# A recurrent attention and a full attention on one core: new order of the segments, paired projection tails, a rebuilt prologue

## The chip, the core and the metric

The kernel runs on one core of one Trainium2 chip. The metric is the time of one execution on the device in microseconds (us). The kernel before takes 1615.6 us (median of 4 runs, 1615.0 to 1619.6).

## The reference, cut to what matters

```python
# A: 64 segments of 32 tokens, one after the other; 8 memory tokens go from each to the next
for s in range(n_seg):
    h = concat([mem, x[s*32:(s+1)*32]])              # 40 tokens x 576
    q, k, v = h @ Wq, h @ Wk, h @ Wv                 # 32 heads of 128
    p = softmax(where(mask, q @ k.T * scale, -1e9))
    o = (p @ v) @ Wo
    mem = o[:8]; outs.append(o[8:])
# B: full attention over all 2048 tokens, 32 heads of 18
b = softmax(q @ k.T * scale) @ v @ wo
# gate
return g * a + (1 - g) * b,  g = sigmoid((x * gate_w).sum(-1))
```

A is a chain: a segment's memory tokens are known only when the segment before is done. B is a heap of independent work: 512 *steps*, each of 4 concurrent score matmuls, an exponential over 128 x 2048 elements and 4 concurrent value matmuls. The kernel weaves B's steps into A's segments, so that the engines have something to do while A's chain waits.

The last 8 tokens of a segment depend on no memory, so their queries, keys and values can be made early. These *last tokens* are done for 16 segments at a time, in 24 units, two of which (2.2 us) go into a segment; four times (for segments 0, 16, 32 and 48), so that none is left to do in the last 16 segments. Every fourth segment has *group work* in those places instead, the output rows of four segments.

## The kernel before

Each segment is a list of names, which are the matmul groups, copies and activations in the order of issue. `B` issues a step's scores and the values of the step before, `E` the exponential; `Q0` to `V1` are the six projections, `t` transposes, `S` scores of A, `x n p l r m` the parts of its softmax, `w` the weighing, `a` the output projection, `f` and `ht` the fold into the memory, `F0` to `F2` the places for last tokens or group work, `c...` and `o...` copies out of PSUM, `v0 v1` the stores of the values. `/` and `:` are places where B's divisions go.

```python
ORDERS = {
    7: """
    Q0 cQ0 K0 B E : cK0 / K1 tq0 tk0 pq0 V0 cK1 B E : pk0 Q1 S0 cV0 v0 cQ1 x0 tk1 n0 B E : tq1 pk1
    V1 pq1 p0 cV1 v1 l0 r0 / S1 m0 B F1 w00 x1 n1 o00 F2 cF1 p1 w01 E : B l1 cF2 o01 r1 m1 E : F0
    a00 w10 cF0 w11 B E : o10 o11 ol a01 a10 a11 B / E : h0 g0 h1 g1 f0 ht0 f1 ht1 og oh
    """.split(),
    8: """
    Q0 B E : V0 cQ0 K0 cV0 v0 B / cK0 E : tq0 pq0 Q1 tk0 pk0 cQ1 B / E : S0 K1 tq1 x0 cK1 B n0 tk1 E
    : V1 pk1 pq1 p0 cV1 v1 S1 l0 r0 x1 / B E : F0 m0 n1 w00 o00 F1 cF0 p1 w01 o01 cF1 l1 r1 m1 B F2
    a00 cF2 w10 o10 w11 E : B E : o11 ol a01 a10 h0 a11 g0 B h1 g1 f0 E : f1 ht0 ht1 oh og
    """.split(),
}
...
LOAD_LAST = "r1"       # in the last segment the loads of the last phase are issued behind this name
...
width = 8 if s >= n_seg - eights else 7      # 28 segments of seven steps, then 36 of eight
```

A projection is five rows of four concurrent matmuls. The fifth row has only 64 of 128 input rows filled, the rest is zero:

```python
def project(x, w, b, k):
    pv = bank(k, [P, 512], FP32, "pvv")
    for c in range(NF + 1):                   # 4 full chunks of 128 and the tail
        for j in range(4):
            rw, cc = w_slice(w, c, (2 * (j // 2) + b) * 1024 + (j % 2) * 512, 512)
            nc.tensor.matmul(pv[32 * j:32 * j + 32, :], lhsT=ht[:, cc, :], rhs=rw,
                             start=(c == 0), stop=(c == NF), tile_position=(0, 32 * j))
```

PSUM is tight: B's scores have four of the eight banks in one buffer, its sums one, and all of A's groups share three, by a table (`BANKS`) that goes with each order. A step's scores therefore can't start before the exponential of the step before has read the buffer.

The softmax here doesn't subtract the row's maximum and nothing guards it: scores larger than these inputs give would overflow.

## Time and profile before

The profiled execution spans 1613.9 us. Its stages, with the lines of the profile, stand in the prediction.

### The profile page before, as it was taken

The numbers are of one execution on the slowest core, as the hardware profiler recorded it, in microseconds if no ns is written. First come the engines' busy times: TensorE is split into PE (matmuls) and PEld (weight loads), VectorE is DVE, ScalarE is ACT, GpSimd is POOL, SyncE is SP. The second block draws the span as 40 slices with busy tenths as digits, with TensorE's granted clock in tenths as the row PEclk, the third lists the DMA queues.
The fourth block names the chain that finished last, engine by engine and source line by source line (L and its number), as shares of the span: only waits on it lengthen the run. The fifth ranks groups of instructions, "written<-read, shape, count | busy, mean of one in ns | idle before, by whom it ended". The sixth has DMA issues, their size and how long they took to land.

```text
span 1613.9 us, 57766 instructions
## 1 busy us (share of the span) xinstructions
PE 1476.7 (91%) x25082; PEld 782.0 (48%) x25082; DVE 960.0 (59%) x2355; ACT 1139.8 (71%) x981; POOL 338.4 (21%) x731
## 2 busy tenths in 40 slices
PE   6598899999999999999999999999999989998997
PEld 3434444555454444555454445555554444444445
DVE  2233666666566666666566666666666656565656
ACT  2165577777677767777677777777777777788774
POOL 6311211213131031302121211212121212120131
PEclk9899999999999999999999999999999999999999
DMA  7788322212122121212122121212221121211125
GB/s 200 235 291 290 100 65 64 49 42 52 45 50 53 32 53 38 61 36 49 43 43 60 38 50 40 57 39 45 51 53 35 30 48 34 45 34 35 29 59 162
DMA packets 209865, 114.39 MB, mean 71 GB/s; under 512 B 159491, under 2 KB 197251, under 8 KB 208019
## 3 DMA queue, kind: packets, MB, share of 16 engines
q1 hardware_dynamic: 188971, 58.40, 16.1%
q0 software_dynamic: 19696, 50.02, 9.9%
q8 instruction: 196, 3.21, 0.9%
q10 hardware_dynamic: 944, 2.29, 0.4%
q14 instruction: 58, 0.48, 0.1%
HBM read 60.94 MB, written 36.10 MB: 60 GB/s over the span
## 4 chain that ended last, share of the span: by engine, by line
PE 69%; ACT 11%; DVE 11%; DMA 4%; issue 2%; SPq 1%; POOL 1%; DVEq 0%; ACTq 0%; POOLq 0%
PE pvv L755 27%; ACT etb L257 9%; PE sb L238 8%; PE ob L222 7%; PE pt L782 5%; PE pv L326 4%; PE psh L800 3%; PE acc L643 3%; PE pso L838 3%; PE pv L313 2%; DVE hl L657 2%; PE pq L420 2%; DVE hl L654 2%; DVE ot L850 2%; ACT rq L830 2%
## 5 line engine op out<-in xcount | busy, mean ns | idle before, releaser
L257 ACT ACTIVATE etb<-sb 128x2048 bf16<-128x2048 f32 x512 | 959.6, 1874 | 341.9 <-PE sb L238 341.1
L767 DVE CAST tm<-pvv 128x512 bf16<-128x512 f32 x384 | 264.4, 689 | 175.1 <-PE pvv L755 174.2
L755 PEld LDWEIGHTS <-ht 128*32 128x32 bf16 x7680 | 185.8, 97 | 183.7 <-DVE ht L891 14.1
L238 PE MATMUL sb<-qch,kch 32*128 32x512 bf16 x2048 | 203.2, 386 | 38.5 <-ACT etb L257 36.7
L222 PE MATMUL ob<-etb,vch 128*32 128x512 bf16 x2048 | 205.9, 392 | 3.9 <-DVE tq L159 3.9
L850 DVE CAST ot<-pso 128x320 bf16<-128x320 f32 x256 | 120.7, 488 | 104.2 <-PE pso L838 99.9
L643 PE MATMUL acc<-wo,ot 128*32 128x384 bf16 (+1 forms) x4096 | 159.7, 291 | 5.4 <-DVE ot L850 3.3
L755 PE MATMUL pvv<-wq_m,ht 128*32 128x512 bf16 x2048 | 134.2, 382 | 13.0 <-DVE ht L891 8.3
L755 PE MATMUL pvv<-wk_m,ht 128*32 128x512 bf16 x2048 | 134.9, 384 | 0.0
L755 PE MATMUL pvv<-wv_m,ht 128*32 128x512 bf16 x2048 | 134.3, 382 | 0.0
L643 PEld LDWEIGHTS <-ot 128*32 128x32 bf16 x4096 | 105.2, 98 | 46.5 <-DVE ot L850 12.8
L700 POOL DMA_DIRECT2D a_dram<-rl x186 | 92.6, 506 | 162.4 <-DVE rl L695 143.3
L238 PEld LDWEIGHTS <-kch 32*128 32x128 bf16 x2048 | 61.2, 91 | 128.5 <-issue 107.9
L857 POOL COPY otl<-ot 128x256 bf16<-128x256 bf16 x64 | 25.9, 405 | 445.6 <-DVE ot L850 445.6
L222 PEld LDWEIGHTS <-vch 128*32 128x32 bf16 x2048 | 52.9, 93 | 120.6 <-issue 116.0
L782 PE MATMUL pt<-ident,tm 128*128 128x128 bf16 x1024 | 96.8, 221 | 0.8 <-DVE tm L767 0.8
L790 DVE COPY kt<-pt 128x512 bf16<-128x512 bf16 x128 | 54.0, 422 | 69.4 <-PE pt L782 69.0
L838 PE MATMUL pso<-et,v_sb 64*128 64x40 bf16 x2048 | 81.4, 178 | 14.9 <-DVE hll L657 4.7
L838 PEld LDWEIGHTS <-v_sb 64*128 64x128 bf16 x2048 | 62.8, 93 | 62.4 <-issue 49.5
L654 DVE CAST hl<-acc 128x384 bf16<-128x384 f32 (+1 forms) x128 | 57.9, 452 | 58.1 <-PE acc L643 57.8
L782 PEld LDWEIGHTS <-tm 128*128 128x128 bf16 x1024 | 57.8, 98 | 67.0 <-issue 49.4
L826 ACT ACTIVATE lt<-pss 128x320 f32<-128x320 f32 x128 | 56.0, 438 | 43.2 <-PE pss L822 32.8
(141 smaller groups left out, 1847.4 us busy)
## 6 DMA issues: line engine op xcount, KB each, us to landing
v_sb<-tm SPq DMA_DIRECT2D x512, 32.0 KB
wo<-in_A_Wo_dram POOLq DMA_DIRECT2D x4, 1152.0 KB, 9.7
wv_m<-in_A_Wv_dram POOLq DMA_DIRECT2D x4, 1024.0 KB, 8.0
wq_m<-in_A_Wq_dram POOLq DMA_DIRECT2D x4, 1024.0 KB, 9.1
wk_m<-in_A_Wk_dram POOLq DMA_DIRECT2D x4, 1024.0 KB, 8.0
xl<-qld SPq DMA_DIRECT2D x64, 64.0 KB
xl<-kld SPq DMA_DIRECT2D x64, 64.0 KB
v_sb<-vld SPq DMA_DIRECT2D x128, 32.0 KB
```

What stands on the lines that cost most here:

```text
L222: nc.tensor.matmul(ob[32 * j:32 * j + 32, :], lhsT=vc[:, o + 32 * j:o + 32 * j + 32], rhs=et4[:, j, :], start=(kb == 0), stop=(kb == NKB - 1),
L238: nc.tensor.matmul(sb[:, j, :], lhsT=kc[32 * j:32 * j + 32, o:o + P], rhs=qch[gq][32 * j:32 * j + 32, :], start=True, stop=True, tile_posi ...
L257: nc.scalar.activation(out=before[:, :, :], in_=sb[:, :, :], func=ACT.Exp, scale=scale_b)
L326: nc.tensor.matmul(pv[:, o:o + P], lhsT=lw, rhs=xlb[:, cc, :], start=(c == 0), stop=(c == NF))
L643: nc.tensor.matmul(acc[32 * j:32 * j + 32, 0:d1 - d0], lhsT=o[:, h, 0:CT], rhs=wo[:, h, d0:d1], start=(b == 0 and i == 0), stop=(b == 1 an ...
L654: nc.vector.tensor_copy(out=hl[:, 0, d0:d1], in_=acc[:, 0:d1 - d0])
L700: eng.dma_start(out=rows4[m, seg - LO:seg, i * n:(i + 1) * n], in_=rl[32 * i + m * LO:32 * i + (m + 1) * LO, :],)
L755: nc.tensor.matmul(pv[32 * j:32 * j + 32, :], lhsT=ht[:, cc, :], rhs=rw, start=(c == 0), stop=(c == NF), tile_position=(0, 32 * j),)
L767: nc.vector.tensor_copy(out=sbt[x][:, :], in_=ps[x][:, :])
L782: nc.tensor.transpose(out=pt[:, which, :, :, :].rearrange("p j (u i) t -> p j u i t", i=4)[:, :, :, i, :], in_=sbt[x][:, i * Dh:(i + 1) * Dh],
L838: nc.tensor.matmul(pso[:, i * L:(i + 1) * L], lhsT=v_sb[64 * jj:64 * jj + 64, b * 1024 + i * Dh:b * 1024 + (i + 1) * Dh], rhs=et[64 * jj:6 ...
L850: nc.vector.tensor_copy(out=ot[:, j * HG:(j + 1) * HG, :].rearrange("p h t -> p (h t)"), in_=ps["o", b, jj][:, 0:W8],)
```

## The change

Its intent: let PE do less (three tails in place of six), fill the prologue, put eight-step segments where there are last tokens, and give the last 16 segments, which have none, an order of their own. The diff, cut to its core (not shown: key and query storage by block, hence plain loads of 18 rows a head; the same value matmuls in four column tiles; the new bank tables; setup moved earlier):

```diff
+        def project_tails(two):
+            two = [(x, w, b, begin(x)) for x, w, b in two]
+            for j in range(4):
+                for x, w, b, first in two:
+                    t, r = w_tail(w, columns(b, j), 512)
+                    nc.tensor.matmul(
+                        ps[x][32 * j:32 * j + 32, :],
+                        lhsT=ht[TL * r:TL * r + TL, NF + r, :],
+                        rhs=t[TL * r:TL * r + TL, :],
+                        start=first, stop=(not first),
+                        tile_position=(TL * r, 32 * j), ...
+                    )
...
-        if spare[0] >= 1.8:
-            spare[0] -= 1.8
+        if spare[0] >= 2.15:
+            spare[0] -= 2.2
...
-    for kb in range(NKB):
+    for kb in range(NKB // 2):
         project_vb(1, kb, 3)
-    for blk in (1, 6, 2, 7, 3, 8):
+    for i, blk in enumerate((1, 6, 2, 7, 3, 8)):
         for t in range(NQC):
             project_qk(blk, t, 0)
             between(1.1)
-        store_qk(blk, range(GB))
+            if i > 0:
+                some_tokens()
+            else:
+                for kb in range(NKB // 2 + 2 * t, NKB // 2 + 2 * t + 2):
+                    project_vb(1, kb, 3)
+        store_qk(blk)
...
+        8: """
+        Q0 B T0 K1 E : / cQ0 T1 cK1 B Q1 E : K0 B V0 cQ1 cK0 T2 tk0 E : tq0 B V1 / cV0 v0 pk0 E : pq0
+        tk1 tq1 cV1 v1 pq1 S0 pk1 B x0 / F1 E : n0 S1 p0 x1 cF1 n1 l0 F2 p1 r0 m0 w00 B cF2 l1 o00 r1 F0
+        m1 w01 w11 cF0 o01 E : w10 o11 o10 ol a00 B a01 E : a10 h0 a11 B g0 h1 f0 g1 ht0 f1 ht1 E : og
+        oh
+        0: """
+        / Q0 T0 B K0 cQ0 Q1 E : T1 cK0 B cQ1 E : K1 V0 cK1 B T2 E : V1 tk0 / / cV0 v0 B E : cV1 v1 tq0
+        pk0 tk1 pq0 tq1 S0 pk1 x0 pq1 S1 n0 F1 p0 x1 l0 cF1 F2 n1 p1 B r0 m0 cF2 l1 F0 cF0 r1 m1 w00 w01
+        E : w10 o00 o01 w11 o10 a00 o11 ol B a01 h0 E : g0 a10 a11 h1 g1 B f0 ht0 E : f1 ht1 og oh
...
-    LOAD_LAST = "r1"
+    LOAD_LAST = [n for n in ORDERS[0] if n[0] in "QKVT"][-1]      # V1
...
-        width = 8 if s >= n_seg - eights else 7
+        width = 8 if s < wides else 7 if s < n_seg - SG else 0     # 41 of eight, 7 of seven, 16 of the third
```

`T0`, `T1`, `T2` are the paired tails. The new seven-step order is left out here.

## The prediction

> **What bounds the kernel now.** I read the page first (engine shares, the chain that ended last), then the busy time by stage, then the PE's own timeline in one segment and in the prologue. The page says that the matmul engine is the bound, with short hand-overs to ScalarE and VectorE:
>
> ```profile
> PE 1476.7 (91%) x25082; PEld 782.0 (48%) x25082; DVE 960.0 (59%) x2355; ACT 1139.8 (71%) x981; POOL 338.4 (21%) x731
> ...
> PE 69%; ACT 11%; DVE 11%; DMA 4%; issue 2%; SPq 1%; POOL 1%; DVEq 0%; ACTq 0%; POOLq 0%
> ```
>
> By stage (first number the stretch, then the busy time of each engine, granted clock, share of the DMA engines, GB/s):
>
> ```profile
> 53.30:85.70 32.40, 16.44 (x176) 11.68 (x174) 5.53 (x14) 2.59 (x7) 5.44 (x15) 0.74 0.85 277
> 85.70:174.60 88.90, 74.99 (x709) 38.57 (x712) 39.45 (x71) 54.44 (x29) 15.14 (x27) 0.98 0.78 260
> 174.60:789.10 614.50, 577.59 (x10386) 307.41 (x10386) 388.77 (x962) 433.70 (x364) 130.21 (x284) 0.99 0.22 52
> 789.10:1213.00 423.90, 409.66 (x7279) 213.82 (x7283) 265.53 (x663) 327.13 (x266) 87.23 (x190) 1.00 0.21 47
> 1213.00:1558.30 345.30, 314.99 (x5746) 160.32 (x5747) 210.20 (x537) 274.45 (x225) 55.47 (x130) 1.00 0.17 35
> ```
>
> The prologue ends at 174.6, when the first projection of segment 0 starts; 29 of the 512 big exponentials lie before it. Then come 28 segments of seven steps (rows 174.6 to 789.1), and 36 of eight. The median seven-step segment takes 21.35 us, an eight-step one that also computes last tokens (up to 1213) 22.43, one without them 21.47; segments 0 to 62 take 1383.7 together, and segment 63 with the ending 55.6. So a segment with one step fewer is hardly shorter, and one without last tokens (2.2 us of matmuls less) gains only 1 us: the work is badly spread, heavy segments fill PE, light ones wait.
>
> The PE timeline of segment 36 gives the prices (start, duration, line, tile, instructions):
>
> ```profile
> 969.32 0.39 PE L755 MATMUL pvv<-wq_t,ht 128*32 128x512 bf16 x4
> 969.64 0.40 PE L238 MATMUL sb<-qch,kch 32*128 32x512 bf16 x4
> 969.97 0.40 PE L222 MATMUL ob<-etb,vch 128*32 128x512 bf16 x4
> 970.19 1.04 PE L755 MATMUL pvv<-wv_m,ht 128*32 128x512 bf16 x16
> 971.05 0.39 PE L755 MATMUL pvv<-wv_t,ht 128*32 128x512 bf16 x4
> 971.27 1.04 PE L755 MATMUL pvv<-wk_m,ht 128*32 128x512 bf16 x16
> ```
>
> Start to start, four concurrent 512-wide matmuls take 0.22 us where the next has the same array shape (971.05 to 971.27), and 0.32 where it has another (969.32 to 969.64). A change of shape costs some 0.105 us. Four rows of a projection take 0.86.
>
> In the prologue PE stands still before it starts the second half of B's values, because the staging buffers' stores stand behind weight loads and per-head stores:
>
> ```profile
> 55.37 7.51 PE L447 MATMUL pvb<-wb,xT 128*128 128x288 bf16 x60
> 78.84 4.73 PE L447 MATMUL pvb<-wb,xT 128*128 128x288 bf16 x20 [15.96 <-DVE xn L291]
> ```
>
> **What the Trainium skill says.** "TensorEngine Tiling (Array Packing)", Tiling Modes, Key Properties: changing the tiling mode, not just the tile, drains TensorE. This trace agrees: 0.105 us a change, as above. The same page, Available Configurations, lists eight independent tiles of 64x32; the paired tails need exactly that, and nothing in this trace uses it. The same page, Gotcha 1, asks that different row tiles write different banks; in all three new bank tables the two projections of a pair do. "ScalarE: Activation LUTs", What ACT_TABLE_LOAD costs, gives 186 ns + 0.833 ns an element, 1892 ns for 2048; the trace has a mean of 1874.
>
> **The change part by part.**
>
> *Paired tails.* A projection's last 64 rows were padded to 128, so six tails of a segment cost six rows of 0.212. Now two projections share the array, upper and lower 64 rows: three rows. That saves 3 x 0.212 = 0.64 us a segment on PE. Each pair adds a shape change or so, up to 3 x 0.105; the sums in four column tiles ([...]in the shape of their neighbours) and the new orders take back more than that.
>
> *Count of PE work.* I listed the groups of each order, priced each by start-to-start distances of the trace (row 0.212; step two rows; four transposes 0.22; scores 0.43 per half; weighing 0.2 per group; output projection 0.65 and 0.33; fold 0.45; last-token unit 1.1) and counted shape changes. Before: seven steps with last tokens 16.8 + 29 x 0.105 = 19.85; eight with them 17.2 + 34 x 0.105 = 20.8; eight without 15.0 + 32 x 0.105 = 18.35. Measured were 21.35, 22.43 and 21.47: 1.5, 1.6 and 3.1 more, waits for DVE and ACT and what the prices miss. After: eight with last tokens 16.55 + about 31 x 0.105 = 19.9; seven with them 16.1 + 28 x 0.105 = 19.05; seven without 13.93 + 26 x 0.105 = 16.7.
>
> *Which segments.* Steps between projections come now each 2.2 units of cost (48 x 1.1 / 2.2 = 24), not 1.8 (29). So 65 - 24 = 41 segments have eight steps, and they come first; 7 have seven; the last 16 use the third order, seven steps without last tokens. Five more eight-step segments is what the shorter prologue costs. The light work now goes where PE has less to do.
>
> *Segment times.* Eight steps: 19.9 plus 1.2 (1.6 before; the order was tuned anew) = 21.1. Seven: 20.4. Last 16: PE needs only 16.7, but a step cannot follow the one before faster than 2.43 us (the pace in the prologue with one projection in between: 88.90 to 91.27 and the like: scores 0.45, exponential 1.87, hand-over), since the scores have one buffer. Seven of those are 17.0; with 1.5 for ACT's six small operations (2.7 us a segment, partly in the gaps) and the chain through the memory I take 18.5, and 20.4 for the every fourth segment that projects the last tokens of four. Segments 0 to 62: 41 x 21.1 + 7 x 20.4 + 4 x 20.4 + 11 x 18.5 = 865 + 143 + 82 + 203 = 1293; 10 us for half-clock stretches and hiccups (the trace has five stretches of 3.4 us at half clock within segments, which cost half of it, some 8 us) make 1303, against 1383.7.
>
> *Prologue.* Up to 53 it stays, minus the pads (a 4 us wait in the chain at 19.5), plus four early weight pieces. Per-head stores become one store a block; the loads become four of 18 rows. Only eight of B's second value blocks come before the first step, fewer than the ring of nine staging buffers, so the 16 us stop goes. From about 62 on PE has 48 units x 1.13 + 8 value blocks x 0.63 + 24 steps x 0.65 = 54 + 5 + 16 = 75 us. It ends near 137; with some waits for DMA I take 141, against 174.6. DMA has some 18.5 MB to move in those 75 us (9.5 of weights, 3 of projections, 2 of values, 3 of last tokens, 1 of loads), 247 GB/s where 260 to 277 was reached, so it isn't far from being the bound.
>
> *Ending.* Segment 63 gets the short order (-2.5), but the 28 last-phase loads are issued earlier on the queue that also stores this segment's values; at 0.4 to 0.5 us an issue I count 6 us of waiting: 59 against 55.6.
>
> Sum: 141 + 1303 + 59 = 1503.
>
> **Rivals.** (1) *Pairs don't run at once.* If the 64x32 tiles of the two halves were serialised, a pair would cost two rows and its shape change stays: 0.64 us x 64 = 41 us worse, 1544. For it: no instruction here shows such tiles; against it: the 32-row and 32-column tiles both run four at a time. (2) *The exponential's cycle becomes the bound.* Eight steps need 8 x 2.43 = 19.4, plus 1.5 to 2.5 for small ACT operations: up to 22 in the 41 heavy segments, +35 us, 1538. The scores waited for ACT only 36.7 us in all before, so there is room. (3) *The prologue is bound by DMA or by memory reuse.* The weights for the output projection are loaded late, without turn-taking, into space that the projections leave; if it all runs at the former pace, the prologue gains only its five steps (5 x 2.9) and part of the 16 us: 155, total 1517. (4) *The new orders wait less.* If excess falls to 0.8 in the heavy segments and to 1 over the exponential pace in the last 16, 25 us fewer: 1478.
>
> **Range and chances.** The prices of PE are firm (they reproduce the segments to the excess), so the gain of tails and changes, some 0.8 us x 64 = 50 us, and about 20 to 33 us of prologue are hard to lose all at once. One rival for the worse gives about 1545, two would give 1580, rival 4 with a good prologue 1465. I say 1503, 1462 to 1546. Faster by over 2% means under 1584: 0.96; within 2%: 0.03; slower: 0.01.
>
> **What would show it.** Tails: eight tail matmuls start to the next group in about 0.32 us with a change, not 0.53. Segments: medians near 21.1 (0 to 40), 20.4, 18.5 (48 to 62). Prologue: 24 exponentials before the first segment's projection, which starts near 141; first exponential near 68, not 86. Ending: in segment 63 weighing waits for the values' transfer. It would be wrong if the 41 heavy segments stay at 22 or over, or PE waits for weights between 70 and 140.

## More of the kernel before

One more line matters later. It is the TensorE clock that was granted, in 40 equal slices of the span, 9 for 90% or more; in the kernel before:

```profile
PEclk9899999999999999999999999999999999999999
```

## The result, and the profile after

The changed kernel takes 1627.9 us (median of 4 runs, 1627.3 to 1632.6), against 1615.6 for the kernel before: a ratio of 1.0077, with a 95% interval of 1.0052 to 1.0102. A ratio here is the one of the runs of the same rounds; it differs from the ratio of the medians quoted by up to 0.11 hundredths. The change makes the kernel a little slower; 1503 had been predicted, and the range ended at 1546.

PE is as busy as before to a tenth of a microsecond, and the chain that ended last runs more over ScalarE:

```profile
PE 1476.6 (91%) x25931; PEld 787.2 (48%) x25946; DVE 953.9 (59%) x2361; ACT 1151.0 (71%) x983; POOL 416.7 (26%) x890
...
PEclk9999999999999999999999999999999788888979
...
PE 61%; ACT 19%; DVE 10%; issue 4%; DMA 3%; POOL 1%; SPq 1%; ACTq 0%; DVEq 0%; POOLq 0%
```

That PE's busy time is the same is an accident: the clock line shows that in the last quarter the clock was granted at less than before, and slow matmuls are busy for longer. The stages (stretch, then PE, weight loads, DVE, ACT, POOL, granted clock, DMA share, GB/s):

```profile
52.50:136.60 84.10, 80.99 (x847) 45.41 (x861) 42.27 (x78) 45.78 (x31) 18.56 (x36) 0.96 0.71 240
136.60:1053.20 916.60, 858.39 (x16174) 462.31 (x16166) 574.51 (x1430) 717.20 (x575) 245.94 (x528) 1.00 0.22 50
1053.20:1202.00 148.80, 138.82 (x2647) 71.15 (x2647) 93.52 (x235) 107.56 (x92) 43.09 (x92) 0.99 0.21 45
1202.00:1559.10 357.10, 313.26 (x5372) 156.26 (x5373) 191.68 (x498) 233.94 (x196) 64.65 (x147) 0.87 0.15 29
1559.10:1625.60 66.50, 43.70 (x569) 27.38 (x569) 33.10 (x77) 30.07 (x45) 11.98 (x23) 0.87 0.43 125
```

The rows are the second part of the prologue, segments 0 to 40, 41 to 47, 48 to 62, and segment 63 with the ending. Against the sum that was predicted:

| | before | predicted | after |
|---|---|---|---|
| prologue | 174.6 | 141 | 136.6 |
| segments 0 to 40 (41 of eight steps) | | 865 | 916.6 |
| segments 41 to 47 (seven steps) | | 143 | 148.8 |
| segments 48 to 62 (third order) | | 285 | 357.1 |
| allowance for the clock and hiccups | | 10 | in the rows above |
| segments 0 to 62 together | 1383.7 | 1303 | 1422.5 |
| segment 63 and the ending | 55.6 | 59 | 66.5 |
| span | 1613.9 | 1503 | 1625.6 |

The prologue gave 38.0 us. The segments took 38.8 back and the ending 10.9 more. The misses of the prediction are 72 us in the last 15 segments, 52 in the heavy ones, 6 in the few of seven steps and 7.5 in the ending; the prologue did 4 us better and the allowance of 10 was counted apart.

*Prologue.* PE is busy for 81.0 of 84.1 us in its second part, where it stood still once for 16 us before. The first of the big exponentials starts at 64.3 (86.1 before), and 24 of them lie before the first projection of segment 0.

*Paired tails.* PE's timeline in segment 22 (start, duration, engine, line, tile, shapes, count):

```profile
632.01 0.40 PE L245 MATMUL ob<-etb,vch 128*32 128x512 bf16 x4
632.34 0.39 PE L821 MATMUL pvv<-wq_t,ht 64*32 64x512 bf16 x1
632.34 0.39 PE L821 MATMUL pvv<-wk_t,ht 64*32 64x512 bf16 x1
...
632.36 0.39 PE L821 MATMUL pvv<-wk_t,ht 64*32 64x512 bf16 x1
632.68 0.61 PE L806 MATMUL pvv<-wk_m,ht 128*32 128x512 bf16 x8
```

All eight start within 0.02 us and the next group follows 0.34 us after the first: eight run at once, as the Trainium skill's page "TensorEngine Tiling (Array Packing)", Available Configurations, lists it for tiles of 64x32. They cost about what a row of four costs with a change of shape (0.32).

*Last segments.* The timeline of PE in segment 57, from the values of the fourth step to those of the fifth; the bracket is the wait before a group and what ended it:

```profile
1426.44 0.40 PE L848 MATMUL pt<-ident,tm 128*128 128x128 bf16 x4
1427.62 0.61 PE L848 MATMUL pt<-ident,tm 128*128 128x128 bf16 x8 [0.78 <-DVE tm L833]
1428.29 0.55 PE L866 MATMUL psh<-qt,kt 128*64 128x40 bf16 x16
1429.69 0.58 PE L866 MATMUL psh<-qt,kt 128*64 128x40 bf16 x16 [0.85 <-DVE qt L856]
1430.20 0.32 PE L889 MATMUL pss<-et,bsel 128*32 128x320 bf16 x4
1431.15 0.32 PE L889 MATMUL pss<-et,bsel 128*32 128x320 bf16 x4 [0.63 <-DVE et L881]
1431.40 0.58 PE L261 MATMUL sb<-qch,kch 32*128 32x512 bf16 x4
```

For 5 us PE has nothing but small groups of A's chain, and waits before most of them. The gap from the fourth exponential to the fifth is 6.16 us, and the next distance 3.95:

```profile
1426.29 1.88 ACT L280 ACTIVATE etb<-sb 128x2048 bf16<-128x2048 f32 x1 [0.56 <-PE sb L261]
...
1432.45 1.86 ACT L280 ACTIVATE etb<-sb 128x2048 bf16<-128x2048 f32 x1
1436.40 1.88 ACT L280 ACTIVATE etb<-sb 128x2048 bf16<-128x2048 f32 x1 [2.10 <-PE sb L261]
```

The scores at 1431.40 last 0.58 us in place of 0.40: the clock has just been granted at half, for 6.83 us, as the record of the clock has it. The same comes back in nearly every one of these segments: 95.6 us at half clock between 1179.9 and 1559.1, where the kernel before has 3.4 in its segments 47 to 62.

*Ending.* In segment 63 (DMA issues of the sync queue, SPq, and matmuls):

```profile
1581.02 5.49 SPq L838 DMA_DIRECT2D v_sb<-tm x8
1584.26 0.81 PE L912 MATMUL pso<-et,v_sb 64*128 64x40 bf16 x16 [9.91 <-DMA v_sb<-tm]
```

The stores of the values are issued only after the loads of the last phase, which now stand before them on that queue, and the weighing waits 9.9 us. The 28 loads are issued from 1561.82 to 1580.84, so in 19.0 us, 0.68 us each with the waits between them.

### The profile page after: what moved, and what is told of

Read it like the earlier page. It is cut to its first block, busy times and chain, and to the rows that moved or that the text cites. A ratio compares the mean times of both kernels' runs of the same rounds, so it can differ in the third digit from the quotient of the medians.

```text
span 1625.6 us, 59693 instructions
## 1 busy us (share of the span) xinstructions
PE 1476.6 (91%) x25931; PEld 787.2 (48%) x25946; DVE 953.9 (59%) x2361; ACT 1151.0 (71%) x983; POOL 416.7 (26%) x890
## 4 chain that ended last, share of the span: by engine, by line
PE 61%; ACT 19%; DVE 10%; issue 4%; DMA 3%; POOL 1%; SPq 1%; ACTq 0%; DVEq 0%; POOLq 0%
ACT etb L280 16%; PE pvv L806 14%; PE sb L261 10%; PE ob L245 6%; PE pv L337 4%; PE acc L685 4%; PE psh L866 4%; PE pt L848 3%; PE pq L442 3%; PE pvv L821 2%; PE accl L685 2%; PE pv L354 2%; DVE tm L833 1%; ACT rq L904 1%; DMA v_sb<-tm 1%
## 5 line engine op out<-in xcount | busy, mean ns | idle before, releaser
L261 PE MATMUL sb<-qch,kch 32*128 32x512 bf16 x2048 | 207.4, 392 | 26.3 <-ACT etb L280 18.0
L806 PEld LDWEIGHTS <-ht 128*32 128x32 bf16 x6144 | 153.3, 96 | 144.9 <-issue 13.0
L245 PE MATMUL ob<-etb,vch 128*32 128x512 bf16 x2048 | 209.7, 399 | 0.9 <-DVE tq L170 0.8
L685 PE MATMUL acc<-wo,ot 128*32 128x384 bf16 (+1 forms) x4096 | 171.6, 316 | 1.6
L261 PEld LDWEIGHTS <-kch 32*128 32x128 bf16 x2048 | 69.3, 91 | 139.4 <-issue 116.2
L924 DVE CAST ot<-pso 128x320 bf16<-128x320 f32 x256 | 114.1, 481 | 20.2 <-PE pso L912 17.4
L848 PE MATMUL pt<-ident,tm 128*128 128x128 bf16 x1024 | 82.0, 220 | 12.9 <-DVE tm L833 12.9
L866 PE MATMUL psh<-qt,kt 128*64 128x40 bf16 x2048 | 74.9, 189 | 15.8 <-DVE qt L856 14.9
L877 ACT ACTIVATE et<-psh 128x320 bf16<-128x320 f32 x128 | 55.9, 437 | 46.8 <-PE psh L866 43.6
```

The costliest lines, as they stand in the source:

```text
L245: nc.tensor.matmul(ob[32 * j:32 * j + 32, :], lhsT=vc[:, o + 32 * j:o + 32 * j + 32], rhs=et4[:, j, :], start=(kb == 0), stop=(kb == NKB - 1),
L261: nc.tensor.matmul(sb[:, j, :], lhsT=kc[32 * j:32 * j + 32, o:o + P], rhs=qch[gq][32 * j:32 * j + 32, :], start=True, stop=True, tile_posi ...
L685: nc.tensor.matmul(acc[32 * j:32 * j + 32, 0:d1 - d0], lhsT=o[:, h, 0:CT], rhs=wo[:, h, d0:d1], start=(b == 0 and i == 0), stop=(b == 1 an ...
L806: nc.tensor.matmul(ps[x][32 * j:32 * j + 32, :], lhsT=ht[:, c, :], rhs=w[0][:, c, columns(b, j):columns(b, j) + 512], start=(first and c = ...
L848: nc.tensor.transpose(out=pt[:, which, :, :, :].rearrange("p j (u i) t -> p j u i t", i=4)[:, :, :, i, :], in_=sbt[x][:, i * Dh:(i + 1) * Dh],
L866: nc.tensor.matmul(psh[64 * jj:64 * jj + 64, i * L:(i + 1) * L], lhsT=kt[:, h * L:h * L + 64], rhs=qt[:, h, :], start=True, stop=True, til ...
```

## The experiments

Each is the changed kernel with the edit named, unless it says otherwise. All gave correct results. They ran on several chips; the runs of the kernel before beside them had medians of 1619.3 to 1622.5, so only ratios to it are compared. A hundredth of it is 16 us. "Half clock" is the time at half clock between the starts of segments 47 and 63. The columns of segments mix kinds: in the kernel before and in e3, e7, e8 and e9, segments 1 to 40 hold both seven-step and eight-step ones and segments 48 to 62 have eight steps; in the others these are eight and seven.

| run | ratio to before (95%) | median us | segments 1 to 40, mean us | 48 to 62, mean us | half clock, us | segment 63 and ending, us |
|---|---|---|---|---|---|---|
| before | 1 | 1615.6 | 22.05 | 21.59 | 3.4 | 55.6 |
| changed | 1.0077 (1.0052 to 1.0102) | 1627.9 | 22.23 | 23.80 | 95.6 | 66.5 |
| e1, loads later | 1.0002 (0.9987 to 1.0017) | 1620.6 | 22.31 | 23.84 | 99.0 | 55.5 |
| e2, idle filled | 1.0038 (1.0022 to 1.0055) | 1625.9 | 22.24 | 23.79 | 20.5 | 66.0 |
| e3, eights last | 0.9830 (0.9814 to 0.9846) | 1592.5 | 21.57 | 22.94 | 75.1 | 68.4 |
| e4, copy first | 0.9987 (0.9972 to 1.0002) | 1618.2 | 21.94 | 23.88 | 99.0 | 66.8 |
| e5, waits filled | 0.9935 (0.9902 to 0.9968) | 1609.6 | 22.28 | 22.31 | 6.8 | 67.8 |
| e6, tails apart | 1.0158 (1.0130 to 1.0187) | 1645.6 | 22.54 | 24.06 | 92.2 | 67.0 |
| e7, old segments | 0.9744 (0.9709 to 0.9779) | 1579.6 | 22.14 | 21.60 | 3.4 | 53.7 |
| e8, by kind | 0.9634 (0.9606 to 0.9663) | 1561.3 | 21.63 | 21.63 | 17.1 | 53.5 |
| e9, a step moved in the eights of e8 | 0.9898 (0.9850 to 0.9946) | 1602.0 | 22.29 | 21.47 | 10.2 | 56.0 |
| e10, a step moved in the third order | 1.0086 (1.0058 to 1.0113) | 1634.2 | 22.25 | 24.20 | 95.6 | 66.0 |
| e11, third order replaced | 0.9784 (0.9768 to 0.9800) | 1588.4 | 22.27 | 20.93 | 17.1 | 68.4 |
| e12, three mended | 0.9640 (0.9618 to 0.9662) | 1564.4 | 22.00 | 20.84 | 17.1 | 58.3 |

**e1: the loads of the last phase behind the values' stores again.**

```diff
-    LOAD_LAST = [n for n in ORDERS[0] if n[0] in "QKVT"][-1]
+    LOAD_LAST = "r1"
```

> The changed kernel, but the loads of the last phase are issued after r1 in the last segment, as before, so behind the stores of its values. Theory (the stores stand in the queue behind 23 loads): the 9.9 us wait of the weighing for v_sb in segment 63 shrinks to under 3 us, segment 63 with the ending goes from 66.5 to about 57, and the whole from 1627.9 to about 1618. Rival (the half-clock stretch at 1575 to 1592 makes the ending slow, or the loads are then missed later): the ending stays at 63 to 67, the whole at 1625 or over.

The ending took 55.5 us in place of 66.5, and the ratio fell by 0.75 hundredths, 12 us. The weighing now waits at most 1.0 us at a time for the values, in place of 9.9, so the place in the queue was the cause of the wait. The time at half clock in that stretch fell with it, from 17.1 to 6.8 us; what that is worth by itself was not separated. (In e12, with late loads too, the ending has 17.2 us at half clock and takes 58.3.)

**e2: useless work where the last tokens have run out.**

```diff
-        next(later, None)
+        if next(later, "none") == "none":
+            spin(k)            # five 512-wide matmuls into a bank that nobody reads
         return lambda: next(later, None)
```

> The changed kernel with useless work added: where the last-token units have run out (the two filler places of segments 47 to 63 that carry no group work) five 512-wide matmuls into a bank that nobody reads. Theory A (the third order leaves PE nearly idle for some 5 us in each segment, the clock is then granted at half for 6.8 us, and that is the larger part of the loss): the granted clock is back at 1.00 in segments 48 to 62, which fall from a mean of 23.8 to about 20.5 to 21.3 although each has about 2 us more PE work; the whole falls by 40 to 55 us to about 1580. Theory B (the chain through the segment is the bound and the half clock is only its companion): the segments stay at 23 to 25 and the whole is 1625 to 1650.

Neither theory as written. The clock came back (20.5 us at half in place of 95.6), as A said, but the segments stayed at 23.8, as B said. The exponentials in segment 57 of this run (two are left out before the first line):

```profile
1424.66 1.88 ACT L280 ACTIVATE etb<-sb 128x2048 bf16<-128x2048 f32 x1 [0.56 <-PE sb L261]
...
1432.47 1.86 ACT L280 ACTIVATE etb<-sb 128x2048 bf16<-128x2048 f32 x1
1435.03 1.88 ACT L280 ACTIVATE etb<-sb 128x2048 bf16<-128x2048 f32 x1 [0.70 <-PE sb L261]
```

The gap between the fourth and the fifth has grown from 6.16 to 7.81 us, because the useless groups stood in A's chain; the distance after it has shrunk from 3.95 to 2.56, because the clock was full. Two effects of the same size hid each other. Hence e5.

**e3: the order of segments as before the change (seven-step first, then eights; no third order).**

```diff
-        width = 8 if s < wides else 7 if s < n_seg - SG else 0
+        width = 7 if s < n_seg - wides else 8
```

> The changed kernel with the order of segments as before the change: 23 seven-step segments first, then 41 of eight, and the third order not used. Nothing else. Theory A (light segments throttle themselves): the last 16 hold eight steps and no last tokens, so PE is busy enough; no half-clock stretches in them, about 21 us each against 23.8; the first 23 take 21.0 (as segments 41 to 46 did with last tokens) against 22.3; the 24 between stay at 22.2. Sum: 23 x 21.0 + 24 x 22.2 + 16 x 21 = 1352, with prologue 136.6 and ending 64 to 67: about 1555. Rival (where steps lie makes no difference, their number does; the loss comes from the new orders themselves): 1610 to 1630.

It gained 40 us, less than the 73 that had been expected. The first 23 segments fell from 22.2 to 21.3, nearly to the 21.0 of the theory. But the eight-step order without last tokens is throttled too. Two neighbours of this run, segment 56 with group work and 57 with neither last tokens nor group work:

```profile
1364.70:1386.90 22.20, 20.96 (x419) 11.16 (x423) 15.45 (x41) 17.54 (x15) 1.33 (x4) 1.00 0.15 29
1386.90:1410.20 23.30, 20.70 (x356) 10.03 (x360) 11.86 (x30) 17.62 (x15) 5.78 (x12) 0.85 0.15 27
```

The segment with 63 matmuls fewer takes 1.1 us longer, at a mean clock of 0.85. Half of the expectation, "PE is busy enough with eight steps", was wrong: in this order the filler places `F1` and `F2` lie in one gap between two steps, so when there is nothing to fill them with, the gap is empty.

**e4: one copy earlier in the eight-step order.**

```diff
-        Q0 B T0 K1 E : / cQ0 T1 cK1 B Q1 E : ...
+        Q0 B T0 K1 E cQ0 : / T1 cK1 B Q1 E : ...
```

> The changed kernel with one move in the eight-step order: the copy of Q0 is issued before the transposes that turn the sums in, not after them. Theory (in every second segment these two transposes, 0.78 us, and the division stand before the copy, and the tails of the second pair, which take Q0's bank, wait 0.785 us for it): the wait goes, the odd ones of segments 1 to 39 fall from 22.5 to about 21.8, 20 x 0.75 = 15 us, the whole to about 1613. Rival (the next step has to wait for the exponential anyway, so PE only waits there instead): odd segments stay within 0.2 us of 22.5, the whole within 4 us of 1627.9.

The odd ones among segments 1 to 39 fell from 22.46 to 21.88, and the ratio by 0.90 hundredths, 15 us, as the theory said. The second pair of tails opens Q1's bank, which is Q0's; in every second segment the two transposes of B's sums and the division stood before the copy that frees it. The lines of segment 23 in the changed kernel:

```profile
654.27 0.78 DVE L170 STREAM_TRANSPOSE tq<-ob 128x256 f32<-128x256 f32 x2 [1.04 <-PE ob L245]
654.49 1.05 PE L806 MATMUL pvv<-wk_m,ht 128*32 128x512 bf16 x16
655.52 0.68 DVE L833 CAST tm<-pvv 128x512 bf16<-128x512 f32 x1
656.25 0.37 PE L821 MATMUL pvv<-wq_t,ht 64*32 64x512 bf16 x1 [0.71 <-DVE tm L833]
```

**e5: useless work only where PE waits anyway.** Three groups of three matmuls in the third order, each in a bank that is free there, in the segments without group work:

```diff
-        ... cV1 v1 tq0 pk0 tk1 pq0 tq1 S0 pk1 x0 pq1 S1 n0 F1 p0 x1 l0 cF1 F2 n1 p1 B
+        ... cV1 v1 tq0 D0 pk0 tk1 pq0 tq1 S0 pk1 x0 pq1 D1 S1 n0 F1 p0 x1 l0 cF1 F2 n1 D2 p1 B
```

> The changed kernel; in the third order three useless groups of three 512-wide matmuls (0.65 us each) are put where PE waits 0.92 to 0.99 us anyway: before the second pair of transposes, before the second scores, before the second sums. The filled-idle run put its 2 us into the chain itself and lengthened the gap between the fourth and fifth exponential from 6.16 to 7.81 us while the clock came back, so it left open what the half clock costs. Theory (half clock costs about 2 us of each of the last segments, the 6.2 us gap in the order the rest): half-clock time in segments 47 to 62 falls from 95.6 us to under 25, the gap stays at 6.2 to 6.6, the segments 48 to 62 fall from 23.8 to about 22.0, the whole by 25 to 30 us. Rival (the clock costs nothing, the chain sets the end): segments stay within 0.4 us of 23.8.

As the theory said: 6.8 us at half clock, the gap in segment 57 at 6.55 us, segments 48 to 62 at 22.31, and the whole 1.42 hundredths, 23 us, *shorter with useless work added*. The stretch of segments 48 to 62 and a little beyond shows the clock of 1.00 (0.87 in the changed kernel):

```profile
1202.00:1559.00 357.00, 320.69 (x5744) 160.86 (x5756) 202.76 (x525) 248.24 (x207) 75.61 (x170) 1.00 0.19 41
```

So the half clock costs 1.5 us of each of these segments. It doesn't explain the other 3.3 us to the 19.0 that were predicted as their mean.

**e6: each projection with its own padded tail again, all else kept.**

```diff
-            for c in range(NF):                 # and project_tails(two) for the rest
+            for c in range(NF + 1):             # project_tails does nothing
```

> The changed kernel with one part undone: each projection computes its own padded tail again (five rows of four), no paired tails; orders, banks and the rest stay. Theory (pairs run eight at once and save 0.64 us less two or three changes of array shape, so 0.3 to 0.4 us of PE a segment, of which the heavy segments keep about half because they wait for the exponential's pace elsewhere): slower than the changed kernel by 8 to 20 us. Rival 1 (waits absorb all): within 4 us. Rival 2 (the early opening of the second bank makes PE wait for the copy of Q0, 0.785 us in every second heavy segment, and costs more than the pair saves): faster by 5 to 15 us.

Slower than the changed kernel by 0.81 hundredths, 13 us; segments 1 to 22 take 22.51 against 22.19. That is the theory's size (0.64 less three changes of shape is 0.33) and its sign: the kernel gains by the pairs. But the trace does not show it as saved work alone. From the changed kernel to this run, in segments 1 to 40, PE is busy 0.10 us a segment more and idle 0.21 more; the wait for Q0's copy, which the pairs brought with them (14.3 us in all, see e4), is gone, and the waits of the scores for the exponential have grown from 14.7 to 40.1 us. What the pairs save PE by themselves is not separated from these moved waits.

**e7: the new prologue; orders, tails, sums and the place of the last loads as before the change** (orders, banks and the placement of the kernel before put back; 23 segments of seven steps, 41 of eight). The loads by head and the last tokens' values in four column tiles stay.

> The new prologue alone: segments, orders, banks, tails, sums, their order (seven-step ones first) and the late loads as before the change; 23 segments of seven steps and 41 of eight. Theory (the prologue's gain of 38 us is real and the five more eight-step segments cost little): prologue 137, segments 1 to 62 as in the kernel before (21.9 and 22.0 mean), ending 55.6: about 2.0 to 2.4% faster than the kernel before (some 1580 where that takes 1616). Rival (what the prologue gains comes back in the first segments, as in segment 0 with 27.5 us, since late weights and stores only move): gain under 1.2%.

2.56 hundredths faster than the kernel before, 41 us, a little over what the theory gave. Segments 1 to 62 are as in the kernel before, so the prologue's gain stays, and all that this run puts back together costs 3.3 hundredths, 54 us. (In the profiled executions the difference to the kernel before is less, 33.0 us: that of this run was the slowest of its four.)

**e8: each kind of segment in the order that suits it.** New prologue; the new seven-step order for segments 0 to 22; the new eight-step order, copy of Q0 first, for 23 to 46; the eight-step order of before with whole tails for the last 17; loads late.

```diff
+        width = 7 if s < n_seg - wides else 8 if s < n_seg - SG - 1 else 9      # 9: eight steps as before
```

> A version put together from what the runs showed: new prologue, the new seven-step order for the first 23 segments (they have last tokens), the new eight-step order with the copy of Q0 first for segments 23 to 46, the eight-step order of before, whose steps lie evenly, with whole tails for the last 17 without last tokens, loads of the last phase late. Theory: 23 x 21.3 + 24 x 21.6 + 16 x 21.5 = 1352 plus 5 for the first segment, 137 and 55.5: about 1550, 4% under the kernel before; no half-clock stretches of note in the last 17. Rival (the old order throttles here too, since what kept it at full clock was not its spacing): last segments 23, whole about 1575.

3.66 hundredths under the kernel before; the theory had 1550 and 4. The last segments run at 21.63 with 17 us at half clock: eight steps, one more than in the third order, in less time.

**e9: on e8, one step of the new eight-step order moved into the gap with the fillers.**

```diff
-        ... n0 S1 p0 x1 cF1 n1 l0 F2 p1 r0 m0 w00 B ... ol a00 B a01 E : a10 h0 a11 B
+        ... n0 S1 p0 B x1 cF1 n1 l0 F2 E : p1 r0 m0 w00 B ... ol a00 a01 a10 h0 a11 B
```

> The put-together version with one step of the new eight-step order moved: from between the output projections into the 4.7 us gap after the fifth exponential, where the two filler units stand. Theory (the steps before and after the gap come at the exponential's own pace of 2.43 us, so PE waits 0.4 to 0.55 us at the step after the output projection, and the gap has room): these waits go, segments 23 to 46 fall from 21.9 to about 21.4, the whole by some 10 us. Rival (ACT does the exponential of the moved step ahead of the logarithm's inverse that the weighing needs, so the chain through the segment gets 1 to 2 us longer): segments 23 to 46 at 22.5 to 23.5, the whole 15 to 35 us longer.

The rival was right: segments 23 to 46 rose from 21.92 to 23.72 us, a little beyond its range, and the whole lost 2.6 hundredths. Waits before the weighing turned up (24.4 us in these 24 segments, where e8 has 3.3), and half-clock stretches with them (78.5 us in segments 0 to 46 in place of 13.7). That fits the rival, an exponential of 1.88 us put before `r0` that holds up the chain; the share of the half clock in the loss was not separated.

**e10: one step of the third order moved into its gap.**

```diff
-        ... E : T1 cK0 B cQ1 E : K1 V0 ...  tq1 S0 pk1 x0 pq1 S1 ...
+        ... E : T1 cK0 cQ1 K1 V0 ...        tq1 B S0 pk1 x0 E : pq1 S1 ...
```

> The changed kernel with one step of the third order moved: the second of the four at its beginning goes to just before the first scores, into the gap of 6.2 us between the fourth and the fifth exponential. No work is added or taken. Theory (the gap is the fault of the order: steps bunched at the beginning, none while the chain of transposes, scores and sums runs; and it calls the half clock): half-clock time in segments 47 to 62 falls from 95.6 to under 40 us, segments 48 to 62 from 23.8 to 21.8 to 22.6, the whole by 15 to 30 us. Rival (the moved exponential stands in front of the chain's small ACT operations and lengthens the chain by what it saves): segments stay at 23.4 or over.

My theory fell here too. The segments took 24.2, the clock stayed as it was, the whole is within the noise of the changed kernel (1.0086 against 1.0077). The wait for the second sums grew, from 0.63 us in segment 57 of the changed kernel to 1.30 in this run. Bunching the steps at the beginning wasn't the fault, or not by itself.

**e11: the third order alone replaced, by the seven-step order of the kernel before with whole tails.** Same number of steps, same segments; the order and banks are those shown under "The kernel before".

> The changed kernel with the third order alone replaced: the last 16 segments run the seven-step order of the kernel before, with whole tails; same number of steps, same place, loads of the last phase still early. Moving a step within the third order had not helped, so what is left is its build: it does all six projections before the first scores, and nothing but the chain of transposes, scores, exponentials and sums stands between the last projection and the weighing, while the old order puts three projections and two steps beside that chain. Theory: segments 48 to 62 at 20 to 21.3 against 23.8, half-clock time there under 30 us, the whole 35 to 55 us shorter, near 1585. Rival (any seven-step order without last tokens starves PE and is throttled): segments 22.5 or over, the whole less than 20 us shorter.

The theory held: segments 48 to 62 at 20.93 (most of those without group work at 20.06), 17.1 us at half clock, and the whole 2.9 hundredths, 47 us, shorter. The stretch, with a clock of 0.98:

```profile
1203.70:1517.70 314.00, 285.48 (x5370) 149.48 (x5370) 195.42 (x495) 229.94 (x195) 64.96 (x147) 0.98 0.17 34
```

**e12: e1, e4 and e11 together.**

> The changed kernel with the three mends that helped singly: loads of the last phase late (13 us), the copy of Q0 first in the eight-step order (15 us), the last 16 segments in the old seven-step order with whole tails (45 us). Theory (the three faults lie in different places and add up): 70 to 75 us under the changed kernel, a ratio to the kernel before of 0.961 to 0.966, as good as the put-together version or slightly better. Rival (mending one moves the wait to another): 0.970 or more.

0.9640: the three add up (12 + 15 + 47 = 74 us; 4.4 hundredths, 71 us, measured). It can't be told from e8, by the intervals. Either beats both kernels by some 58 us or more.

## Why the prediction was wrong

*Right: that pairs run eight at once, and the sign of PE's work.* Eight tiles run at once, the next group comes 0.34 us later where 0.32 had been named, and the kernel is 13 us slower when they are taken apart (e6). PE's busy time in the heavy segments fell from 21.56 us a segment (409.66 us in 28 to 46 before) to 20.88 (835.09 us in 1 to 40 after), by 0.68; the listing had said 0.9.

*Right: the prologue.* 136.6 for 141; 41 us with the segments put back (e7). The third rival, that DMA or memory reuse would hold it up, showed only in segment 0 (27.5 us, with the weighing waiting 2.9 us for the values).

*Right in mechanism, too small: the ending.* "At 0.4 to 0.5 us an issue I count 6 us of waiting": the loads did hold up the values' stores (e1), and the wait was 9.9 us. The term that was mis-sized is the price of an issue: 0.68 us with the waits between. The ending cost 10.9 us more than before in place of 3.4.

*Wrong: what the heavy segments take beyond PE's work.* The step that failed is "Eight steps: 19.9 plus 1.2 (1.6 before; the order was tuned anew) = 21.1". The mean of segments 1 to 40 is 22.23, so 2.3 us came on top of the listing and not 1.2; before it was 1.5 (the mean of 28 to 46, 22.31, less 20.8). The prediction's own sign of being wrong, 22 or over, came true. PE stood idle for 1.35 us a segment, against 0.75 before. I took for granted that an order rebuilt with new banks waits less; it waits nearly twice as much, and most of the 0.68 us of work that was saved went into waiting. About half of the new waiting is the shared bank of Q0 and Q1 (e4 takes 0.29 us a segment away, all of it idle time of PE). Most of the rest is scores that wait for the exponential, the path of the second rival, which said that there was room. The profile's sums of these waits (us, times), for segments 28 to 46 before and 1 to 40 after:

```profile
  ACT etb L257: 1.2, 5
  ACT etb L280: 14.7, 46
```

One try to take them away, a step moved into the gap, made things worse (e9), so I have no order that does it.

*Wrong: "the last 16", 18.5 us without group work.* This is the larger part of the miss, 72 us. The step that failed is "Seven of those are 17.0; with 1.5 for ACT's six small operations [...] and the chain through the memory I take 18.5". I put the floor at seven exponentials at their pace and added 1.5 us for "the chain through the memory". The chain was not such an addition to the steps: in the third order all six projections come before the first scores, four steps are done by then, and the transposes, scores, exponentials, sums and logarithms of both halves stand alone between. What e5 leaves at full clock is 22.31, 3.3 us over the predicted mean of 19.0; e10 shows that a step put there stands in the chain's way; e11 shows that an order with three projections and two steps beside the chain needs 20.93. As e11 changes order, banks and tails together, it shows that the third order was at fault, but not by which trait; that it is the chain left alone is read from the order and from the waits in segment 57. (The pace of 2.43 us was no floor either: the same trace has steps that follow after 2.35 us. That is too little to matter.)

*Missed altogether: the clock.* The allowance of 10 us came from five half-clock stretches of the kernel before. That an order can make PE idle in every segment, and be granted half clock in nearly every one, was in no rival. It cost 1.5 us of each of the last segments (e5), some 23 us. The Trainium skill's page "TensorE: Matmul & The Clock Gate", HAM oscillation, tells of this kind of loss: idle gaps that bring the clock down each time round a loop. Its rule there is to keep gaps under some 3.4 us. The runs agree on the kind (e2, e5: filling the gap brings the clock back). On the size they are less plain: the longest single wait of PE in the gap of segment 57 is 0.85 us, with small groups between, so it isn't a single idle gap of that length that did it here. What exactly sets the grant stays open; I tested filling, not its threshold.

By sums: had the last segments run as in e11, the heavy ones as in e4 and the ending as in e1, the kernel would be at 0.964 (e12), or 1557 where the kernel before takes 1616. The prediction of 1503 would still have been 54 us too low. The largest part of this rest lies in the heavy segments, 22.00 us in e12 where 21.1 had been predicted.

One reading in the prediction is to be put right: 21.35 us is the median of the seven-step segments with last tokens; over all 28 it is 21.57.

## What to carry to other kernels

Work taken from the busiest engine is a gain only if the order around it doesn't wait for something else; when several chains are woven by hand, price the *waits* of the new order from its dependences, and don't let "it was tuned" stand in for that. An order belongs to the load that it was made for: take the fillers out of it and its gap stays, and may bring the clock down. If useless matmuls in a wait make a kernel faster, the clock was part of the cost; put them where they lengthen no chain, or two effects will hide each other.

## What the Trainium skill lacked or had wrong

- "TensorE: Matmul & The Clock Gate", HAM oscillation: it speaks of idle gaps over some 3.4 us. In the third order half clock was granted in nearly every segment, mostly for 6.83 us, after 5 us in which PE worked in small groups, with waits of at most 0.85 us each in segment 57 (95.6 us in all in segments 47 to 62). The page's next section, A second HAM failure mode, does name small idle times between groups of matmuls, but says neither how long they were nor how thinly filled a stretch may be.
- "TensorEngine Tiling (Array Packing)", Key Properties: it says that a change of mode drains TensorE, without a figure. Here a change took 0.105 us, start to start (0.32 against 0.22).
- The same page, Available Configurations, lists eight tiles of 64x32 without a measurement. Here eight 512-wide matmuls in such tiles started within 0.02 us and the next group 0.34 us after the first; taking the three pairs of each segment apart cost 13 us in the whole (e6), moved waits included.
- No page has a measurement of useless matmuls that pay (HAM oscillation advises padding, and measures only its other remedy): 23 us here (e5).
